# Routed experts on one core: where expert 0's early results are kept, when row numbers are converted, and VectorE's turns spread over layer 2

## The chip, the cores and the metric

The kernel runs on one core of one Trainium2 chip. The metric is the device time of one execution in microseconds (us); the median of several runs counts.

## What is computed

Three stages follow each other: sliding-window attention, a gated dense block, and a layer of eight experts of which each token uses one. The change lies in the last stage; there `x` has 2304 rows of 512, `w1[e]` is 512 x 1024 and `w2[e]` is 1024 x 512.

```python
logits = x @ w_gate
e_idx = np.argmax(logits, axis=1)
...
for e in range(E):
    mask = e_idx == e
    h = np.maximum(x[mask] @ w1[e], 0.0)
    ye = h @ w2[e]
    out[mask] = gate_w[mask, None] * eom[mask, e, None] * ye
```

## The kernel before

Every product of two float32 matrices is made from three matmuls: each operand is split into a rounded high part and a low remainder (ScalarE writes the high part, line 470 or 771, VectorE or GpSimd the remainder, line 471 or 775), and high*high, high*low and low*high are summed. So ScalarE and VectorE must split every piece of weights and every block of rows before TensorE can use it.

The router scatters the rows of `x` by expert into a DRAM buffer `xs`, from tiles of a pool `mo` (line 434, indirect DMAs that GpSimd issues). Each expert has a stretch of `xs`; a row carries 512 numbers, its target row in `out` and its weight.

**Expert 0** begins before all rows are routed. Its first 256 rows were fetched early; `static_block` (line 1073) computes layer 1 (`hps`, line 1083) and then layer 2 (`mm2`, line 1053) in two blocks of 128 rows, `j` = 0 and 1. ScalarE scales each block's result into a tile from `y_first` (line 1179, shown in the trace as `gt`), and GpSimd issues an indirect DMA of 256 KB to `out` (line 1049). In a hook within the first block's matmuls, `rest` (line 1182) asks SyncE for the remaining rows of expert 0 (tile `xg`, 128 x 514) and for all four blocks of expert 1's rows (`rows`, line 818): eight DMAs of 128 KB, and one of 4 KB with row numbers and weights, which GpSimd converts to integers (line 804). A pair of row blocks lives in one of three buffers (`pair_tile`, line 792).

Then the pools `mo` and `moe` are closed (line 1195) and a pool `ex2` is opened in the same place in SBUF; `exT`, `hT` and `y` of all later experts live there. The remaining rows of expert 0 are transposed by TensorE (`gps`, line 841), split into `exT`, and go through `row_block` (line 1117): 24 matmuls of layer 1 with the rows as the stationary side (`rps`, line 1136), transposes (`tps`), and 24 matmuls of layer 2.

**Experts 1 to 7** each run a `static_block` of 288 columns: layer 1 is 96 matmuls, layer 2 48. While expert e computes, VectorE and ScalarE prepare e+1: eight weight pieces (`esplit`, line 778, one ScalarE copy and one VectorE subtraction each), and three row blocks, each turned by VectorE (line 850, into a PSUM bank of `ps_s`) and split (lines 470 and 471) into `exT`. `begin` and `turn` (lines 1207 to 1213) take the next row block from a list. ScalarE's and VectorE's order is the order in which the program is written (`manual_schedule`), and hooks after the matmuls of step f of layer 1 (`at1`), of the first block of layer 2 (`at2`) and of the second (`at3`) place this work in it; SyncE's and GpSimd's order around it is a scheduler's. After the two blocks an expert with more than 288 rows runs row blocks, one with 257 to 288 rows runs `few_rows` (line 1101, `yps` of line 1107), one with at most 256 goes straight on.

Of the kernel before, what the change touches and what calls it, by code (L numbers as in the profile page):

```python
# [9 lines left out]
F32 = mybir.dt.float32  # L10
# [11 lines left out]
NT, DM, DF, NE = B * S, H * D, 1024, 8  # L22
NP = H // 2
UNIT = 384
# [4 lines left out]
NS = NT + 128  # L29
# [412 lines left out]
def attention_moe_moe_kernel(ctx: ExitStack, tc: tile.TileContext, q0, k0, v, w1, w2, w3, w_out,  # L442
# [26 lines left out]
    def split(src, hi, lo, low=nc.vector):  # L469
        nc.scalar.activation(out=hi, in_=src, func=AF.Copy)  # L470
        low.tensor_tensor(lo, src, hi.bitcast(F32), op=ALU.subtract)  # L471
# [54 lines left out]
    raw, f32s, bits = {}, {}, {}  # L526
# [87 lines left out]
    mo, ghl = [None], [None]  # L614
# [125 lines left out]
    def eslot(e, i):  # L740
        if ew[e][i] is None:
            j = 0 if e % 2 == 0 else 2 + 2 * i
            ew[e][i] = [wslot(j), wslot(j + 1)]
        return ew[e][i]
# [4 lines left out]
    def eload(to):  # L749
        while nload[0] < min(to, len(items)):  # L750
            e, i, c = items[nload[0]]
            if ex[0] is not None and nload[0] % 4 == 3:
                t = ex[0].tile([128, 1024], F32, name="ck3", tag="ck3", bufs=1)
            else:
                t = exp_state["p"].tile([128, 1024], F32, name="ck2", tag="ck2", bufs=3)
            if i == 0:
                nc.sync.dma_start(out=t, in_=ew1[e, 128 * c:128 * c + 128, :])
            else:
                nc.sync.dma_start(out=t.rearrange("p (a d) -> p a d", a=2),
                                  in_=ew2[e, 256 * c:256 * c + 256, :].rearrange("(a p) d -> p a d", p=128))  # L760
            eq.append(t)
            nload[0] += 1
# [7 lines left out]
    def ehigh():  # L770
        nc.scalar.activation(out=eparts()[0], in_=eq[0], func=AF.Copy)  # L771

    def elow(low=V):
        hi, lo = eparts()
        low.tensor_tensor(lo, eq.popleft(), hi.bitcast(F32), op=ALU.subtract)  # L775
        nsplit[0] += 1

    def esplit(low=V):
        if nsplit[0] < len(items):
            ehigh()  # L780
            elow(low)
            eload(nsplit[0] + (3 if ex[0] is None else 4))
# [7 lines left out]
    idx, xg, xTs = {}, {}, {}  # L790

    def pair_tile():
        return exp_state["p"].tile([128, 1024], F32, name="xg", tag="xg", bufs=3)

    def blocks(t, r, n):

        o = t.rearrange("p (j c) -> p j c", c=128)
        for b in range(4):
            nc.sync.dma_start(out=o[32 * b:32 * b + 32],
                              in_=xs[r:r + 128 * n, 128 * b:128 * b + 128].rearrange("(j p) c -> p j c", p=32))  # L800

    def fetch_index(raw, i, r, n):
        nc.sync.dma_start(out=raw[:, 0:n], in_=xs[r:r + 128 * n, DM:RW].rearrange("(j p) t -> p j t", p=128))
        nc.gpsimd.tensor_copy(i[:, 0:n], raw[:, 0:n, 0])
# [6 lines left out]
    def index(e, pool=None, tag="idx", bufs=5):  # L811
        p = pool or exp_state["p"]
        t = p.tile([128, 12], F32, name="idx", tag=tag, bufs=bufs)
        raw = t[:, 4:12].rearrange("p (j t) -> p j t", t=2)
        idx[e] = (t[:, 0:4].bitcast(I32), raw[:, :, 1])
        return raw

    def rows(e):

        raw = index(e)  # L820
        for j in (0, 2):
            t = pair_tile()
            blocks(t, NS * e + 128 * j, 2)
            xg[e, j], xg[e, j + 1] = t[:, 0:512], t[:, 512:1024]
        fetch_index(raw, idx[e][0], NS * e, 4)

    def early_rows():

# [15 lines left out]
    def xT_block(g, xT, c0, ab=False):  # L844
        split(g_turn(g, ab), xT[:, 0, :, c0:c0 + 128], xT[:, 1, :, c0:c0 + 128])

    def xT_square(g, xT, c0):

        ps = ps_s.tile([128, 512], F32, name="gps", tag="S")
        V.transpose(out=ps, in_=g)  # L850
        h, lo = [xT[:, b, :, c0:c0 + 128].rearrange("p c (a j) -> p c a j", a=4) for b in range(2)]
        split(ps.rearrange("p (a c j) -> p c a j", a=4, c=4), h, lo)

    def early_turn(j):
        if j == 0:
# [197 lines left out]
    def mm2(hT, c0, w, hooks={}):  # L1053
        ps = ps_acc.tile([128, 512], F32, name="yps", tag="acc")
        for f in range(8):
            for i, (a, b) in enumerate(PASSES):
                mm(ps, lhsT=hT[f][a][:, c0:c0 + 128], rhs=w[b][:, 512 * f:512 * f + 512],  # L1057
                   start=f == 0 and i == 0, stop=f == 7 and i == 2)
            if f in hooks:
                hooks[f]()  # L1060
        return ps
# [55 lines left out]
    def row_block(xT, ix, j, w1e, w2e, own, then={}):  # L1117
        hs, hT = [], {}

        def turn(z):  # L1120
            tp = ps_s.tile([128, 512], F32, name="tps2", tag="S")
            for f in range(4):
                nc.tensor.transpose(tp[:, 128 * f:128 * f + 128], hs[z][:, 128 * f:128 * f + 128], ident)
            tp = tp.rearrange("p (a b) -> p a b", a=4)
            for f in (0, 2):
                h2 = own[4 * (j % 2) + 2 * z + f // 2][4][:, 0:512].rearrange("p (a b c) -> p a b c", a=2, b=2)
                split(tp[:, f:f + 2, :], h2[:, 0], h2[:, 1])
                for i in range(2):
                    hT[4 * z + f + i] = h2[:, 0, i], h2[:, 1, i]

        for z in range(2):
            ps = (ps_s if z else ps_v).tile([128, 512], F32, name="rps", tag="S" if z else "pv")
            for kk in range(4):
                c = 1024 * kk + 512 * z
                for i, (a, b) in enumerate(PASSES):
                    mm(ps, lhsT=xT[:, a, kk, 0:128], rhs=w1e[b][:, c:c + 512],
                       start=kk == 0 and i == 0, stop=kk == 3 and i == 2)
                if z and kk == 1:
                    turn(0)
            h = ex[0].tile([128, 512], F32, name="hs", tag="y", bufs=3)  # L1140
            nc.scalar.activation(out=h, in_=ps, func=AF.Relu)
            hs.append(h)
        ps = mm2(hT, 0, w2e, {1: lambda: turn(1), **then})
        emit_out(ps, ix, j)
# [25 lines left out]
    hold = {}  # L1170
# [6 lines left out]
        return h[:, 0], h[:, 1]  # L1177

    def y_first():
        return mo[0].tile([128, 2, UNIT], F32, name="gt", tag="gt", bufs=2).rearrange("p a b -> p (a b)")[:, 0:DM]  # L1180

    def rest():

        n0 = nc.values_load(rt.done[0:1, 0:1], min_val=0, max_val=256)
        index(0)
        xg[0, 0] = pair_tile()[:, 0:RW]
        nc.sync.dma_start(out=xg[0, 0], in_=xs[bass.ds(n0, 128), :])
        rows(1)

    at1 = {k: lambda n=n: step(n) for k, n in {(0, 2): 1, (1, 0): 1, (1, 2): 1, (2, 0): 1, (2, 2): 1, (3, 0): 3, (4, 3): 3, (5, 0): 3}.items()}  # L1190
    at1.update({f: lambda: esplit(nc.gpsimd) for f in ((0, 0), 1, (2, 1))})
# [12 lines left out]

    steps = deque()

    def turn():
        if steps:
            xT_square(*steps.popleft())

    def begin(e):
        steps.extend(prep(e))
        turn()

    w1e, w2e = eslot(0, 0), eslot(0, 1)
    n0 = nc.values_load(rt.done[0:1, 0:1], min_val=0, max_val=256)
    n = nc.values_load(rt.cnt[0:1, 0:1], min_val=0, max_val=NT)
    xT = ex[0].tile([128, 2, 4, 384], F32R, name="exT", tag="exT", bufs=2)[:, :, :, 256:384]
    own = [h_tile(f) for f in range(8)]
# [3 lines left out]
    written = ExitStack()  # L1223
    written.enter_context(tc.manual_schedule(engines={E.DVE, E.Activation}))
    xT_block(xg[0, 0], xT, 0)
    row_block(xT, idx[0], 0, w1e, w2e, own, {2: lambda: begin(1), 4: turn, 6: turn})
    for e in range(1, NE):
        at1 = {f: esplit for f in (0, 2, 4, 6)}
        at3 = {3: esplit, 6: esplit}
        if e + 1 < NE:  # L1230
            rows(e + 1)
            at3.update({0: lambda e=e: begin(e + 1), 2: turn, 5: turn})
        reg = {}

        def ahead():
            reg["n"] = nc.values_load(rt.cnt[0:1, e:e + 1], min_val=0, max_val=NT)  # L1236
            reg["lots"] = reg["n"] > EW

        def tell(label, cond):
            tc.mark_branch_hint_location(label, hint=cond, engines={E.PE})  # L1240

        at2 = {1: esplit, 2: ahead, 5: esplit, 7: lambda: tell(f"lots{e}", reg["lots"])}
        hT = static_block(e, idx[e], at1, at2, at3)
        w1e, w2e = eslot(e, 0), eslot(e, 1)
        n, lots = reg["n"], reg["lots"]
        xT = xTs.pop((e, 2))
        with tc.If(lots, label=f"lots{e}") as rest_of:
            more = n > 384
            tell(f"more{e}", more)
            row_block(xT[:, :, :, 256:384], idx[e], 2, w1e, w2e, hT, {3: lambda: xT_square(xg[e, 3], xT, 0)})  # L1250
            with tc.If(more, label=f"more{e}"):  # L1251
                row_block(xT, idx[e], 3, w1e, w2e, hT)
                with tc.If(n > 512):  # L1253
                    row_loop(e, 512, n, w1e, w2e, xT, hT)
        with rest_of.Else():
            with tc.If(n > 256):
                few_rows(hT, idx[e], w2e)
# [55 lines left out]
```

## Time and profile before

| what | value |
|---|---|
| three runs | 744.34, 745.35, 746.1 us |
| median | 745.35 us |
| the profiled execution | 742.05 us |
| its span, first to last instruction | 740.1 us |
| TensorE (PE) busy | 703.5 us, 95% |
| VectorE (DVE) / ScalarE (ACT) busy | 396.0 us, 54% / 306.4 us, 41% |
| GpSimd (POOL) busy | 152.4 us, 21% |
| the same page's clock row | full, but for two slices of 40 near 480 to 520 us |

Times in the trace are us from the start of the span. In a line of the timeline stand: start, duration, engine, source line, operation, out<-in, count, and in brackets how long the engine was idle before and what ended that. SPq is SyncE's DMA queue, PEq the sequencer of TensorE.

### The profile page before, as it was taken

The page shows a single profiled execution, that of the slowest core. Times are in us where ns is not written, and L with a number is a line of the kernel's source. Part 1 is how long each engine was busy: PE and PEld are TensorE (multiplying, and loading weights), DVE is VectorE, ACT ScalarE, POOL GpSimd, SP SyncE. Part 2 cuts the span into 40 slices and gives each one's busy share as a digit, 9 for nine tenths or more (in the row PEclk, how much of TensorE's full clock was granted, in tenths as well). Part 3 has the DMA queues.
Part 4 walks back from the last instruction along what each step waited for, and adds up shares of the span by engine and source line. Part 5 has one row for each costly group of instructions (what it writes and reads, how often), then busy time and mean ns, then how long its engine had stood idle before and what let it go on. Part 6 is the DMA issues. An engine that isn't in the chain of part 4 may idle for free. (4 is left out here: it accounts for less than half of the span.)

```text
span 740.1 us, 12043 instructions
## 1 busy us (share of the span) xinstructions
PE 703.5 (95%) x4423; PEld 627.8 (85%) x4423; DVE 396.0 (54%) x882; ACT 306.4 (41%) x707; POOL 152.4 (21%) x183
## 2 busy tenths in 40 slices
PE   7999999999999999999999999928999999999996
PEld 3788899999999999999999999816997988978985
DVE  7999788214544657364422425603666665566310
ACT  3665656222333435334412215402555554545222
POOL 4764655100310312030010012410011001010111
PEclk9999999999999999999999999968999999999999
DMA  9992699920211432122310024573576876474000
GB/s 355 408 407 92 222 323 265 253 91 0 93 50 33 128 118 96 33 76 86 114 44 0 1 72 122 179 192 82 168 206 197 249 207 200 125 215 138 18 28 30
DMA packets 53285, 105.80 MB, mean 143 GB/s; under 512 B 8524, under 2 KB 22860, under 8 KB 53200
## 3 DMA queue, kind: packets, MB, share of 16 engines
q1 hardware_dynamic: 49952, 95.24, 41.6%
q0 software_dynamic: 3104, 9.46, 3.4%
q8 instruction: 45, 0.74, 0.4%
q14 instruction: 40, 0.33, 0.1%
q10 hardware_dynamic: 144, 0.03, 0.0%
HBM read 86.83 MB, written 18.53 MB: 142 GB/s over the span
## 5 line engine op out<-in xcount | busy, mean ns | idle before, releaser
L622 PE MATMUL ab<-xt,w 128*128 128x384 f32 x1152 | 216.4, 340 | 0.0
L622 PEld LDWEIGHTS ab<-xt,w 128*128 128x128 f32 x1152 | 199.5, 188 | 2.1
L646 PE MATMUL acc<-w,gt 128*128 128x512 f32 x432 | 110.4, 400 | 0.0
L1057 PE MATMUL yps<-w,hT 128*128 128x512 f32 x432 | 101.0, 391 | 0.0
L1057 PEld LDWEIGHTS yps<-w,hT 128*128 128x128 f32 x432 | 80.4, 188 | 16.3
L646 PEld LDWEIGHTS acc<-w,gt 128*128 128x128 f32 x432 | 78.8, 188 | 15.2 <-DVE gt L638 0.2
L630 DVE TENSOR_TENSOR a_sb<-ab,a_sb 128x384 f32<-128x384 f32 x48 | 26.7, 555 | 89.8 <-PE ab L622 84.5
L191 ACT ACTIVATE pp<-sps,nm 128x128 f32<-128x128 f32 x144 | 46.7, 365 | 53.0 <-DVE nm L180 49.0
L213 POOL TENSOR_TENSOR pp<-pp,r 128x384 f32<-128x384 f32 x48 | 40.1, 850 | 118.7 <-DVE r L206 82.6
L775 DVE TENSOR_TENSOR w<-ck,w 128x1024 fp32r<-128x1024 f32 x45 | 54.5, 1224 | 14.0 <-ACT w L771 13.5
L1083 PE MATMUL hps<-exT,w 128*128 128x288 f32 x384 | 53.5, 300 | 5.2 <-ACT exT L470 4.3
L1083 PEld LDWEIGHTS hps<-exT,w 128*128 128x128 f32 x384 | 52.2, 192 | 7.1 <-ACT exT L470 5.1
L1049 POOL DMA_INDIRECT out<-y,idx x18 | 19.2, 1065 | 179.8 <-ACT exT L470 83.9
L771 ACT ACTIVATE w<-ck 128x1024 fp32r<-128x1024 f32 x48 | 49.9, 1055 | 6.7 <-DMA ck<-in_moe_w 6.0
L602 PE MATMUL wps<-w,w3T 128*128 128x512 f32 x192 | 50.3, 405 | 1.2 <-POOL w3T L593 1.0
L634 ACT ACTIVATE gt<-a_sb 128x384 fp32r<-128x384 f32 x48 | 25.1, 522 | 55.7 <-DVE a_sb L630 55.7
L627 ACT ACTIVATE a_sb<-ab 128x384 f32<-128x384 f32 x48 | 23.6, 491 | 55.2 <-PE ab L622 55.2
L1090 DVE SCALAR_TENSOR_TENSOR hT<-hps,hT 128x256 fp32r<-128x256 f32 x112 | 29.1, 301 | 28.4 <-ACT hT L1088 26.5
L1083 PE MATMUL hps<-exT,wx 128*128 128x288 f32 x288 | 41.2, 304 | 3.2 <-ACT exT L470 2.6
L1083 PEld LDWEIGHTS hps<-exT,wx 128*128 128x128 f32 x288 | 40.2, 195 | 4.6 <-ACT exT L470 3.4
L602 PEld LDWEIGHTS wps<-w,w3T 128*128 128x128 f32 x192 | 34.4, 188 | 9.7 <-POOL w3T L593 1.9
L1088 ACT ACTIVATE hT<-hps 128x288 fp32r<-128x288 f32 x56 | 23.0, 411 | 46.2 <-PE hps L1083 44.5
(155 smaller groups left out, 915.6 us busy)
## 6 DMA issues: line engine op xcount, KB each, us to landing
ck<-in_moe_w SPq DMA_DIRECT2D x80, 512.0 KB
q<-in_q SPq DMA_DIRECT2D x16, 576.0 KB
v<-in_v SPq DMA_DIRECT2D x16, 576.0 KB
xs<-x SPq DMA_DIRECT2D x32, 257.0 KB
w<-in_moe_w SPq DMA_DIRECT2D x16, 512.0 KB
xg<-xs SPq DMA_DIRECT2D x56, 128.0 KB
k<-in_k SPq DMA_DIRECT2D x16, 320.0 KB
w<-in_moe_w_out SPq DMA_DIRECT2D x8, 512.0 KB
```

The costliest lines, as they stand in the source:

```text
L191: nc.scalar.activation(out=p[:, o], in_=ps[:, o], func=AF.Exp, bias=nm[:, i:i + 1], scale=0.125, **(dict(accum_out=s["rs"][:, 3 * g + i:3 ...
L213: nc.gpsimd.tensor_tensor(p, p, s.pop(("r", g)).unsqueeze(2).to_broadcast([128, 3, 128]), op=ALU.mult)
L602: mm(ps, lhsT=t[:, a, 128 * j:128 * j + 128], rhs=wo[b][:, o:o + 512], start=g == 0 and j == 0 and x == 0, stop=g == 1 and j == 3 and x == 2)
L622: mm(ps, lhsT=w[a][:, c:c + 128], rhs=x[:, b, kk, :], start=kk == 0 and i == 0, stop=kk == 3 and i == 2)
L630: V.tensor_tensor(asb[u, m], gps.pop((u, m, 1)), asb[u, m], op=ALU.mult)
L634: nc.scalar.activation(out=g[:, 0, :], in_=asb[u, m], func=AF.Copy)
L646: mm(accs[u][t], lhsT=g[:, a, 128 * t:128 * t + 128], rhs=ws["w34"][b][:, 512 * m:512 * m + 512], start=m == 0 and i == 0, stop=m == 7 and ...
L771: nc.scalar.activation(out=eparts()[0], in_=eq[0], func=AF.Copy)
L775: low.tensor_tensor(lo, eq.popleft(), hi.bitcast(F32), op=ALU.subtract)
L1057: mm(ps, lhsT=hT[f][a][:, c0:c0 + 128], rhs=w[b][:, 512 * f:512 * f + 512], start=f == 0 and i == 0, stop=f == 7 and i == 2)
L1083: mm(ps[:, 0:W], lhsT=w1e[a][:, c:c + 128], rhs=xT[:, b, kk, 0:W], start=kk == 0 and i == 0, stop=kk == 3 and i == 2)
L1090: nc.vector.scalar_tensor_tensor(out=lo, in0=ps[:, o], scalar=0.0, in1=h[0][:, o].bitcast(F32), op0=ALU.max, op1=ALU.subtract)
```

## The change

Five edits go together.

1. `y_first` takes one pair tile of the pool of row tiles (128 x 1024, both early results) in place of tiles of `mo`. That pool stays open when `mo` closes.
2. `rows` takes one pair of blocks at a time and no longer asks for the row numbers. `rest` asks for expert 1's first pair alone; the second pair, in the buffer of the early results, and the numbers are asked for after expert 0's remaining rows were split.
3. `numbers` fetches and converts row numbers, after both pairs.
4. Expert 1's first two blocks are turned and split ahead of expert 0's row block, the third in the hook at f=2 of its layer 2 (before: all three, at f=2, 4 and 6).
5. For experts 2 to 7 the three turns move from `at3` (f = 0, 2, 5) to `at2` f=1, `at2` f=5 and `at3` f=1, each with a weight split between the turn and the split of its block. The two weight splits of `at3` move from f=3 and 6 to f=1 and 5.

```diff
-    def rows(e):
-        raw = index(e)
-        for j in (0, 2):
-            t = pair_tile()
-            blocks(t, NS * e + 128 * j, 2)
-            xg[e, j], xg[e, j + 1] = t[:, 0:512], t[:, 512:1024]
-        fetch_index(raw, idx[e][0], NS * e, 4)
+    def rows(e, j):
+        if j == 0:
+            index_of[e] = index(e)
+        t = pair_tile()
+        blocks(t, NS * e + 128 * j, 2)
+        xg[e, j], xg[e, j + 1] = t[:, 0:512], t[:, 512:1024]
+    def numbers(e):
+        fetch_index(index_of[e], idx[e][0], NS * e, 4)
...
     def y_first():
-        return mo[0].tile([128, 2, UNIT], F32, name="gt", tag="gt", bufs=2).rearrange("p a b -> p (a b)")[:, 0:DM]
+        if "y" not in hold:
+            hold["y"] = pair_tile()
+            return hold["y"][:, 0:DM]
+        return hold["y"][:, DM:2 * DM]
...
-        rows(1)
+        rows(1, 0)
...
-    def turn():
-        if steps:
-            xT_square(*steps.popleft())
     def begin(e):
         steps.extend(prep(e))
-        turn()
+    def turn(n=1, sp=False):
+        todo = [steps.popleft() for _ in range(n)]
+        ps = [square(t[0]) for t in todo]
+        if sp:
+            esplit()
+        for p, t in zip(ps, todo):
+            halves(p, *t[1:])
...
     xT_block(xg[0, 0], xT, 0)
-    row_block(xT, idx[0], 0, w1e, w2e, own, {2: lambda: begin(1), 4: turn, 6: turn})
+    rows(1, 2)
+    numbers(1)
+    begin(1)
+    turn(2)
+    row_block(xT, idx[0], 0, w1e, w2e, own, {2: turn})
...
-        at3 = {3: esplit, 6: esplit}
+        at3 = {1: esplit, 5: esplit}
         if e + 1 < NE:
-            rows(e + 1)
-            at3.update({0: lambda e=e: begin(e + 1), 2: turn, 5: turn})
+            rows(e + 1, 0)
+            rows(e + 1, 2)
+            numbers(e + 1)
+            begin(e + 1)
+            at3[1] = lambda: turn(1, True)
...
-        at2 = {1: esplit, 2: ahead, 5: esplit, 7: lambda: tell(f"lots{e}", reg["lots"])}
+        at2 = {1: esplit, 2: ahead, 5: esplit} if e + 1 == NE else {1: lambda: turn(1, True), 2: ahead, 5: lambda: turn(1, True)}
```

`square` is VectorE's turn and `halves` the two splits, which stood together in `xT_square`.

**GpSimd at the end of expert 0.** The first two rows take the row numbers from expert 0's remaining rows, line 804 converts an expert's numbers, and the line below it with `out` sends the two early results. Before:

```order
L808 CAST idx<-xg 128x1
L809 COPY idx<-xg 128x1
L804 CAST idx<-idx 128x4
L1049 DMA out<-gt,idx 2304x512 x2
L804 CAST idx<-idx 128x4
L1216 TENSOR_LOAD done
```

Now:

```order
L808 CAST idx<-xg 128x1
L809 COPY idx<-xg 128x1
L1059 DMA out<-xg,idx 2304x512 x2
L1232 TENSOR_LOAD done
L1236 REGISTER_ALU
```

The conversion of expert 1's numbers no longer stands ahead of the early results, nor expert 2's behind them; both now come after the branch.

**SyncE from expert 0's remaining rows (line 1187, now 1200) to expert 2's first weights.** `ck` are weight pieces, `xg` row blocks, `idx` numbers. Before, ahead of the branch:

```order
L1187 DMA xg<-xs 128x514
L799 DMA xg<-xs 32x8x128 x8
L803 DMA idx<-xs 128x4x2
L757 DMA ck_5104<-in_moe_w 128x1024
L757 DMA ck_5117<-in_moe_w 128x1024
L757 DMA ck_5130<-in_moe_w 128x1024
L803 DMA idx<-xs 128x4x2 x2
```

Now, ahead of the branch and (from the second `x4` on) behind it:

```order
L1200 DMA xg<-xs 128x514
L799 DMA xg<-xs 32x8x128 x4
L757 DMA ck_5097<-in_moe_w 128x1024
L757 DMA ck_5110<-in_moe_w 128x1024
L757 DMA ck_5123<-in_moe_w 128x1024
...
L799 DMA xg<-xs 32x8x128 x4
L803 DMA idx<-xs 128x4x2
L799 DMA xg<-xs 32x8x128 x8
L803 DMA idx<-xs 128x4x2
L757 DMA ck_5473<-in_moe_w 128x1024
```

Expert 1's second pair and its numbers moved behind three weight pieces and the branch, and both pairs of expert 2 now stand ahead of the weight piece `ck_5473`, which came first there.

**VectorE in layer 2 of expert 1.** Before:

```order
L775 TENSOR_TENSOR w_5616<-ck_5475,w_5615 128x1024
L1236 TENSOR_LOAD cnt
L775 TENSOR_TENSOR w_5616<-ck_5513,w_5615 128x1024
L850 STREAM_TRANSPOSE gps<-xg 128x512
L471 TENSOR_TENSOR exT<-gps,exT 128x4x128
L850 STREAM_TRANSPOSE gps<-xg 128x512
L471 TENSOR_TENSOR exT<-gps,exT 128x4x128
L775 TENSOR_TENSOR w_5616<-ck_5551,w_5615 128x1024
L850 STREAM_TRANSPOSE gps<-xg 128x512
L471 TENSOR_TENSOR exT<-gps,exT 128x4x128
L775 TENSOR_TENSOR w_5616<-ck_5589,w_5615 128x1024
```

Now:

```order
L854 STREAM_TRANSPOSE gps<-xg 128x512
L775 TENSOR_TENSOR w_5618<-ck_5475,w_5617 128x1024
L471 TENSOR_TENSOR exT<-gps,exT 128x4x128
L1259 TENSOR_LOAD cnt
L854 STREAM_TRANSPOSE gps<-xg 128x512
L775 TENSOR_TENSOR w_5618<-ck_5513,w_5617 128x1024
L471 TENSOR_TENSOR exT<-gps,exT 128x4x128
L854 STREAM_TRANSPOSE gps<-xg 128x512
L775 TENSOR_TENSOR w_5618<-ck_5551,w_5617 128x1024
L471 TENSOR_TENSOR exT<-gps,exT 128x4x128
L775 TENSOR_TENSOR w_5618<-ck_5589,w_5617 128x1024
```

Each turn now stands ahead of a weight split and its block's split behind it, and the first turn is ahead of all four weight splits of the layer.

## Rows read from the trace of the kernel before

**Rows 1.** Waits of TensorE: us in total, times, longest.

```profile
PE rps L1136 <- ACT exT L470: 14.3, 1, 14.3
PE hps L1083 <- ACT exT L470: 6.9, 4, 3.0
```

**Rows 2.** Timeline of all engines, end of expert 0.

```profile
480.33 4.33 SPq L799 DMA_DIRECT2D xg<-xs  x8
...
482.68 0.69 ACT L1048 ACTIVATE gt<-yps,idx 128x512 f32<-128x512 f32 x1 [2.26 <-PEq L1220]
483.00 0.19 POOL L808 CAST idx<-xg 128x1 int32<-128x1 f32 x1 [8.11 <-DMA xg<-xs]
...
483.08 0.63 PE L841 MATMUL gps<-ident,xg 128*128 128x128 f32 x4 [0.52 <-DMA xg<-xs]
...
489.17 0.19 POOL L804 CAST idx<-idx 128x4 int32<-128x4 f32 x1 [5.86 <-DMA idx<-xs]
489.93 1.01 POOL L1049 DMA_INDIRECT out<-gt,idx  x1 [0.57 <-issue]
494.45 0.98 POOL L1049 DMA_INDIRECT out<-gt,idx  x1 [3.51 <-DMA out<-gt,idx]
...
497.31 0.60 ACT L470 ACTIVATE exT<-gps 128x512 fp32r<-128x512 f32 x1 [13.95 <-DMA out<-gt,idx]
```

**Rows 3.** Timeline of TensorE, experts 1 to 6 and one row block.

```profile
514.51 0.55 PE L1083 MATMUL hps<-exT,w 128*128 128x288 f32 x1 [3.00 <-ACT exT L470]
...
529.11 11.06 PE L1057 MATMUL yps<-w,hT 128*128 128x512 f32 x48
...
556.44 11.08 PE L1057 MATMUL yps<-w,hT 128*128 128x512 f32 x48
...
582.15 11.05 PE L1057 MATMUL yps<-w,hT 128*128 128x512 f32 x48
...
609.52 11.08 PE L1057 MATMUL yps<-w,hT 128*128 128x512 f32 x48
620.44 4.36 PE L1136 MATMUL rps<-wx,exT 128*128 128x512 f32 x18
...
633.02 12.91 PE L1083 MATMUL hps<-exT,w 128*128 128x288 f32 x96 [0.43 <-PEq L1251]
645.77 11.06 PE L1057 MATMUL yps<-w,hT 128*128 128x512 f32 x48
...
671.62 11.05 PE L1057 MATMUL yps<-w,hT 128*128 128x512 f32 x48
```

**Rows 4.** One stretch: length, TensorE busy, granted clock, DMA share, GB/s.

```profile
498.00:503.50 5.50, 5.50 (x18) 0.73 0.88 192
```

**Rows 5.** Timeline of SyncE's queue: two loads of row blocks.

```profile
511.87 1.79 SPq L799 DMA_DIRECT2D xg<-xs  x4
...
544.04 3.32 SPq L799 DMA_DIRECT2D xg<-xs  x5
```

**Rows 6.** A stretch: length, PE, PEld, DVE, ACT, POOL busy, clock, DMA share, GB/s.

```profile
515.50:516.00 0.50, 0.50 (x3) 0.50 (x4) 0.00 (x0) 0.00 (x0) 0.50 (x1) 0.50 0.00 0
```

**Rows 7.** Groups by line: turns and splits, busy us and mean ns.

```profile
L775 DVE TENSOR_TENSOR w<-ck,w 128x1024 fp32r<-128x1024 f32 x45 | 54.5, 1224 | 14.0 <-ACT w L771 13.5 <-issue 0.4
L771 ACT ACTIVATE w<-ck 128x1024 fp32r<-128x1024 f32 x48 | 49.9, 1055 | 6.7 <-DMA ck<-in_moe_w 6.0 <-PE ab L622 0.8
L471 DVE TENSOR_TENSOR exT<-gps,exT 128x512 fp32r<-128x512 f32 x24 | 16.6, 692 | 41.7 <-ACT exT L470 41.7
L850 DVE STREAM_TRANSPOSE gps<-xg 128x512 f32<-128x512 f32 x23 | 16.5, 718 | 0.0
L470 ACT ACTIVATE exT<-gps 128x512 fp32r<-128x512 f32 x24 | 14.3, 596 | 40.0 <-DVE gps L850 21.9 <-DMA out<-gt,idx 13.9 <-issue 4.2
```

**Rows 8.** Timeline of layer 2 of expert 2: copy of the third block.

```profile
568.16 0.60 ACT L470 ACTIVATE exT<-gps 128x512 fp32r<-128x512 f32 x1 [1.93 <-DVE gps L850]
```

**Rows 9.** Waits of SyncE's queue: us in total, times, longest.

```profile
SPq L757 <- DMA out<-gt,idx: 8.1, 1, 8.1
```

More of the change, by code (lines that the diff above doesn't have):

```diff
@@ L816, in index @@
         return raw
-    def rows(e):
-        raw = index(e)
-        for j in (0, 2):
-            t = pair_tile()
-            blocks(t, NS * e + 128 * j, 2)
-            xg[e, j], xg[e, j + 1] = t[:, 0:512], t[:, 512:1024]
-        fetch_index(raw, idx[e][0], NS * e, 4)
+    def rows(e, j):
[6 more added lines that the diff above has]
+        fetch_index(index_of[e], idx[e][0], NS * e, 4)
+    index_of = {}
     def early_rows():
@@ L845, in xT_block, with square, halves, xT_square @@
         split(g_turn(g, ab), xT[:, 0, :, c0:c0 + 128], xT[:, 1, :, c0:c0 + 128])
-    def xT_square(g, xT, c0):
+    def square(g):
         ps = ps_s.tile([128, 512], F32, name="gps", tag="S")
         V.transpose(out=ps, in_=g)
+        return ps.rearrange("p (a c j) -> p c a j", a=4, c=4)
+    def halves(ps, xT, c0):
         h, lo = [xT[:, b, :, c0:c0 + 128].rearrange("p c (a j) -> p c a j", a=4) for b in range(2)]
-        split(ps.rearrange("p (a c j) -> p c a j", a=4, c=4), h, lo)
+        split(ps, h, lo)
+    def xT_square(g, xT, c0):
+        halves(square(g), xT, c0)
     def early_turn(j):
@@ L1240, in tell @@
             tc.mark_branch_hint_location(label, hint=cond, engines={E.PE})
-        at2 = {1: esplit, 2: ahead, 5: esplit, 7: lambda: tell(f"lots{e}", reg["lots"])}
+        at2 = {1: esplit, 2: ahead, 5: esplit} if e + 1 == NE else {1: lambda: turn(1, True), 2: ahead, 5: lambda: turn(1, True)}
+        at2.update({7: lambda: tell(f"lots{e}", reg["lots"])})
         hT = static_block(e, idx[e], at1, at2, at3)
```

## The prediction

> **What bounds the kernel now.** TensorE is busy 95% of the span by the page's first part, so I first ask where it stands still, in the view of the waits. Two lines hold nearly all of it [rows 1]: one wait of 14.3 us of `rps`, the first matmul of expert 0's row block, and four waits of 6.9 us together of `hps`, the first matmul of a layer 1. Both wait for ScalarE's copy into `exT`. The next view is the timeline around the long wait [rows 2]. TensorE's transposes of expert 0's remaining rows end at 483.08 + 0.63 = 483.71, but the ScalarE copy that reads them begins at 497.31, and what ended its wait is named: the DMA from `gt` to `out`, an early result. The reader should follow that back. The tile of the copy lies in the pool opened over the closed one, so it can't be written before the early results have left. They left late: ScalarE had written them by 482.68 + 0.69 = 483.37, but GpSimd issued the first at 489.93, because ahead of it in GpSimd's queue stood the conversion of expert 1's row numbers (489.17), which waited 5.86 us for its load. The second went out only when the first had landed, 4.52 us later, and landed 2.86 us after that.
>
> The third view is the timeline of TensorE alone [rows 3]. With no wait, layer 2 and layer 1 of a 288-column expert take 620.44 - 609.52 = 10.92 and 645.77 - 633.02 = 12.75, together 23.67 us from one layer 2 to the next. The short waits stand at the starts of experts 1, 3, 4 and 6; behind experts 1, 4 and 6 a `few_rows` or a row block hides the preparation of the next. The last view is the granted clock [rows 4]: 0.73 on the mean in the 5.5 us after the long wait, that is partly the lower level of 1.2 GHz, so a wait costs more than its own length.
>
> **The change part by part.** Expected from here: the start of `hps` of expert 1 (514.51), then its layer 1, then the transitions.
>
> *Early results in an open pool, conversions later.* The wait of the copy for the early results goes. Next in line are TensorE's transposes (483.71) and ScalarE's second early result (483.37), then a branch on ScalarE whose cost no row shows. TensorE took the same branch and began its transposes 0.4 us after its sequencer had released ScalarE (482.68 to 483.08 [rows 2]); between 0 and 0.9 I take 0.3 past 483.71. So the copy begins near 484.0, takes 0.60, and TensorE starts at 484.65.
>
> The row block takes 12.15 us at the full clock (633.02 - 0.43 - 620.44). But two turns and splits of expert 1 now stand ahead of it on VectorE and ScalarE, and its second half writes into a PSUM bank that the first of them uses. It comes after 12 of 24 matmuls, 484.65 + 12 x 0.24 = 487.5. The first turn needs its rows: four DMAs from 480.33 [rows 2]. Four such DMAs elsewhere were issued from 511.87 on, and by 515.5 no data moved [rows 5, 6], so 4.0 us from first issue to landing; with the 257 KB copy ahead of them I take 485.0. At worst it is 489.17, when the numbers loaded behind them were in. Two turns and two splits, alternating, then end at 485.3 + 2 x 0.72 + 2 x 0.69 = 488.1, the first split at 487.5 [rows 7]: no wait, or up to 3.6 us at worst. The ScalarE copy of the row block's own result is due behind them at 487.5 and is not late.
>
> The third block is loaded into the buffer of the early results, so SyncE must wait until both have landed. GpSimd issues the first at 483.4 (after the conversion at 483.00), the second 4.5 us later, and that lands 2.9 to 4.5 us later: 490.8 to 492.4, I take 491.3. Four loads land 4.0 us after, 495.3; turn 0.72, copy 0.60 and subtraction 0.69 make the block's two parts ready at 496.7 and 497.4. The row block ends at 484.65 + 12.15 = 496.8. So `hps` runs properly from 497.3 instead of 514.51: **17.2 us**, at least 12, at most 18. The Trainium skill (DMA: Bandwidth & Descriptors, section Anatomy of one DMA — SWDGE (gpsimd) path) gives 2.0 us and bytes over 436e3 for such a copy: by an estimate from it, 2.6 us for each early result, and the third block would be ready 2.8 us sooner, so that the row block's end alone counts and the gain is 17.7. The rows' 4.52 and 2.86 are longer, and I keep them.
>
> Behind that wait SyncE now holds the other loads: 1 index load, 8 blocks and the weight piece `ck_5473`. At 0.45 us of issue each (1.79 for four [rows 5]) that piece is issued at about 497.5. Its split is the last of four in expert 1's layer 1, some 11 us after 497.3, so this costs nothing; if the wait were 8 us longer it would begin to. The numbers of expert 1 are needed when its first block leaves, 18 us after 497.3.
>
> *Expert 1's layer 1* took 529.11 - 514.51 = 14.6, against 12.75 without the lower clock [rows 3]: **1.85 us**, none if TensorE still pauses there.
>
> *Turns spread over layer 2.* The three transitions without cover, from layer 2 to next layer 2, took 582.15 - 556.44 = 25.71, 609.52 - 582.15 = 27.37 and 671.62 - 645.77 = 25.85 [rows 3], 2.04, 3.70 and 2.18 over 23.67: **7.9 us** in all. The third block's copy ended at 568.16 + 0.60 = 568.76 there [rows 8], 12.3 after the layer's start. Now, from that start: VectorE is free at about 1.7, after the last weight split of layer 1 (1.22) and some 0.5 for the last `hT`; each of three rounds is a turn, a weight split and a block's split, 0.72 + 1.22 + 0.69 = 2.63 [rows 7], and ScalarE's 1.06 + 0.60 for a round fit beside it, its copy of the first output (due at 5.6) too. Three rounds end at 9.6, before the layer's 10.92, and the fourth weight split follows at 10.9, where nobody waits yet. So all of the excess should go; between 0 and 7.9 I take 7.9. The cover of this is the rows' early landing: the first turn is now wanted at 1.7, ahead of the weight splits. The loads of the block wanted first at 558.1 were issued from 544.04 to 547.36 [rows 5] and land 2.3 us after the last issue, 549.6, so 8.5 us are left.
>
> No arithmetic and no DMA is added.
>
> **The sum.** 17.2 + 1.85 + 7.9 = 27.0 us. The profiled execution took 742.05, its span 740.1; it becomes 715.0. The median of the runs shown is 3.3 above the profiled one, and I subtract the same from it: 745.35 - 27.0 = 718.4 us.
>
> **The rivals.**
>
> *The row block is late.* The first rows land near their bound of 489.17, or the early results take 4.5 us each and the third block comes late, and the clock falls again. For it: DMA queues are full in this stretch, and the third block's chain ends within 0.6 us of the row block's. Cost 3 to 6 us: 721 to 724.
>
> *The spread turns don't pay.* VectorE's row is in order; if something else there is late, the transitions stay as they are: 745.35 - 19.1 = 726.3. Against it: 1.3 us of slack in the sum above.
>
> *The change doesn't do what it says:* the copy into `exT` still waits, for the routed rows' scatter that also leaves the closed pool. Then 17.2 and 1.85 go, but for the third block's 3.0: 745.35 - 7.9 - 3.0 = 734.5. Against it: the load of the remaining rows, which reads what that scatter wrote, was already in at 483.00 [rows 2].
>
> *Slower: SyncE's queue holds the rows.* Place: the first turn in `at2`, in each of the six transitions. A SyncE load that waits for a buffer holds all loads behind it; it waited 8.1 us in one piece for the early results [rows 9]. If rows come after the turn is wanted, VectorE stands, the weight splits behind the turn stand with it, and TensorE waits for both. It decides from 8.5 + 1.3 = 9.8 us later than in the trace on; to eat 27.0 and 1.5 more over six transitions each must be 4.8 beyond that: about 747 us. For it: the turns are wanted earlier, and the loads have moved behind weight pieces. Against it: the weight splits also end earlier, and their loads with them. The Trainium skill (DMA: Bandwidth & Descriptors, section Anatomy of one DMA — SWDGE (gpsimd) path) says that a wait on a semaphore is held by the issuing sequencer before dispatch, which is this mechanism; by that the trace's 8.1 us agree.
>
> **How the numbers follow.** The forecast has 0.72, by itself 715.5 to 721. The late row block has 0.12, the turns that don't pay 0.08, the copy that still waits 0.05, slower 0.03. The range reaches from 714.5 (18 in place of 17.2, a lower clock nowhere, and some 2 us of spread between runs) to 726.5, which takes in the first two rivals and leaves out 0.08 and the tails. No change means within 0.2% of 745.35, about what a measurement of this kernel can tell; only mixtures with the last rival fall there, 0.02. So faster 0.95, slower 0.03.
>
> **What would show it.** Right: TensorE's list of waits has no `rps` entry above 1 us; GpSimd issues the first early result near 483.4; `hps` of expert 1 starts near 497; the clock stays full from 480 to 525; the starts of layer 2 of experts 2, 3 and 4 lie 23.7 apart; the chain's tail is as long as before. Wrong: a wait of `rps` on VectorE's split, of VectorE's turn on a DMA in layer 2, or of a weight split on its piece.

## The result, and the profile after

The changed kernel takes **723.68 us** (median of 6 runs, 722.26 to 725.11); the kernel before took 745.73 in the same comparison (6 runs, 742.43 to 747.35). The ratio is 0.9708, with an interval of 0.9681 to 0.9735: 22 us faster. The forecast of 718.4 was 5.3 too low; its range of 714.5 to 726.5 held the time. What came is the price of the first rival, the late row block (721 to 724). The profiled execution took 725.11, its span is 723.1, so by profile against profile the gain is 742.05 - 725.11 = 16.9; the profiled execution of before was 3.3 quicker than its median, that of the changed kernel 1.4 slower.

The page's first line, busy time by engine, has TensorE at 97% of a shorter span; the work itself is the same.

```profile
PE 703.1 (97%) x4423; PEld 628.5 (87%) x4423; DVE 393.8 (54%) x882; ACT 307.1 (42%) x707; POOL 151.8 (21%) x183
```

The long wait is gone from TensorE's list of waits, and what is left of the two entries of before [rows 1] is this:

```profile
PE hps L1093 <- ACT exT L470: 2.7, 1, 2.7
PE rps L1146 <- ACT exT L470: 1.5, 1, 1.5
PE rps L1146 <- DVE exT L471: 0.2, 1, 0.2
```

The timeline of all engines of the changed kernel at the end of expert 0 answers to [rows 2] (start, duration, engine, line, operation, and in brackets the idle time and what ended it):

```profile
482.16 1.90 SPq L799 DMA_DIRECT2D xg<-xs  x4
484.17 1.65 SPq L757 DMA_DIRECT2D ck<-in_moe_w  x3
484.50 0.69 ACT L1058 ACTIVATE xg<-yps,idx 128x512 f32<-128x512 f32 x1 [2.66 <-PEq L1236]
...
484.91 0.63 PE L845 MATMUL gps<-ident,xg 128*128 128x128 f32 x4 [0.50 <-DMA xg<-xs]
...
485.59 1.00 POOL L1059 DMA_INDIRECT out<-xg,idx  x1 [0.45 <-ACT xg L1058]
486.35 0.60 ACT L470 ACTIVATE exT<-gps 128x512 fp32r<-128x512 f32 x1 [1.16 <-PE gps L845]
...
488.38 1.32 DVE L854 STREAM_TRANSPOSE gps<-xg 128x512 f32<-128x512 f32 x2 [0.70 <-DMA xg<-xs]
...
493.67 0.98 POOL L1059 DMA_INDIRECT out<-xg,idx  x1 [7.08 <-ACT hT L470]
...
496.41 1.81 SPq L799 DMA_DIRECT2D xg<-xs  x4
...
501.21 0.73 DVE L854 STREAM_TRANSPOSE gps<-xg 128x512 f32<-128x512 f32 x1 [3.58 <-DMA xg<-xs]
```

ScalarE's copy into `exT` no longer waits for a DMA to `out`: it begins 0.81 after TensorE's transposes end (485.54). But the two early results, sent by GpSimd at 485.59 and 493.67, lie 8.08 us apart, where they lay 4.52 apart before [rows 2]. What ends the second one's wait there, by the trace's inference, is a ScalarE copy (`hT`) that had ended at 493.10. I read it as the first one's landing: the traces of before [rows 2] and of the closed pool below name that DMA at the same place. SyncE loads expert 1's third block behind both, from 496.41 on, and VectorE waits 3.58 us for it.

The timeline of TensorE alone, for [rows 3]:

```profile
502.62 16.13 PE L1093 MATMUL hps<-exT,w 128*128 128x288 f32 x96 [2.70 <-ACT exT L470]
518.58 11.06 PE L1067 MATMUL yps<-w,hT 128*128 128x512 f32 x48
...
545.91 11.08 PE L1067 MATMUL yps<-w,hT 128*128 128x512 f32 x48
...
559.12 11.22 PE L1093 MATMUL hps<-exT,w 128*128 128x288 f32 x84 [0.16 <-issue]
570.17 11.08 PE L1067 MATMUL yps<-w,hT 128*128 128x512 f32 x48
...
594.28 11.05 PE L1067 MATMUL yps<-w,hT 128*128 128x512 f32 x48
...
630.49 11.07 PE L1067 MATMUL yps<-w,hT 128*128 128x512 f32 x48
...
654.59 11.04 PE L1067 MATMUL yps<-w,hT 128*128 128x512 f32 x48
```

And stretches of TensorE (length, busy, granted clock, DMA share, GB/s): from the copy to the row block's end, the pause, and expert 1's layer 1.

```profile
486.00:490.50 4.50, 3.33 (x12) 1.00 1.01 327
490.50:499.90 9.40, 9.38 (x44) 1.00 0.39 112
499.90:502.60 2.70, 0.01 (x1) 0.95 1.16 206
502.60:512.00 9.40, 9.27 (x47) 0.65 0.81 187
```

From these lines the gain splits as the prediction's sum did:

| piece | before | after | gain | forecast |
|---|---|---|---|---|
| start of `gps` | 483.08 | 484.91 | -1.83 | 0 |
| `gps` to `hps` of expert 1 | 31.43 | 17.71 | 13.72 | 17.2 |
| expert 1's layer 1 | 14.60 | 15.96 | -1.36 | 1.85 |
| three uncovered transitions | 78.93 | 72.47 | 6.46 | 7.9 |

The sum is 16.99, against 16.94 of the two executions. The first line lies ahead of the change: the last scatter of the routed rows is already issued 1.85 us later in this execution (474.74 against 472.89), and the kernels below have the start of `gps` between 483.1 and 484.9. The tail is as it was: from the last of these starts of layer 2 to the end of the span 68.5 in both.

### The profile page after: what moved, and what is told of

Same layout as the page of the kernel before. It is cut to its first block, busy times and chain, and to the rows that moved or that the text cites. A ratio compares the mean times of both kernels' runs of the same rounds, so it can differ in the third digit from the quotient of the medians.

```text
span 723.1 us, 12045 instructions
## 1 busy us (share of the span) xinstructions
PE 703.1 (97%) x4423; PEld 628.5 (87%) x4423; DVE 393.8 (54%) x882; ACT 307.1 (42%) x707; POOL 151.8 (21%) x183
## 5 line engine op out<-in xcount | busy, mean ns | idle before, releaser
L775 DVE TENSOR_TENSOR w<-ck,w 128x1024 fp32r<-128x1024 f32 x45 | 54.7, 1217 | 12.6 <-ACT w L771 12.2
L602 PE MATMUL wps<-w,w3T 128*128 128x512 f32 x192 | 52.5, 419 | 2.3 <-ACT w3T L589 1.3
L1059 POOL DMA_INDIRECT out<-y,idx x18 | 17.6, 976 | 161.2 <-ACT y L1058 110.2
L602 PEld LDWEIGHTS wps<-w,w3T 128*128 128x128 f32 x192 | 36.1, 197 | 11.3 <-POOL w3T L593 1.9
L168 PE MATMUL sps<-k,q 128*128 128x128 f32 x288 | 40.5, 280 | 1.1 <-DMA k<-in_k 1.1
L168 PEld LDWEIGHTS sps<-k,q 128*128 128x128 f32 x288 | 38.0, 194 | 3.9 <-issue 1.7
```

Source lines behind the costliest of these rows:

```text
L168: nc.tensor.matmul(ps[:, 128 * i:128 * i + 128], lhsT=s["q"][:, 128 * c:128 * c + 128], rhs=s["k"][:, 64 * c:64 * c + 128], start=late, st ...
L602: mm(ps, lhsT=t[:, a, 128 * j:128 * j + 128], rhs=wo[b][:, o:o + 512], start=g == 0 and j == 0 and x == 0, stop=g == 1 and j == 3 and x == 2)
```

## The experiments

Theory after the result: the open pool and the spread turns work as forecast, and what is missing comes from the first early result, which takes long to land because SyncE's loads, now issued around it, share the DMA engines with it. Expert 1's third block is loaded behind it, so TensorE pauses and its clock falls. Rivals: the landing time is the scatter's own; the pool is not what matters; the spread turns don't pay.

All runs in one table. Issue is when GpSimd issued the two early results; the last three columns are pieces of the profile, as above. The first four were compared with 745.23 (median of 13 runs), the last four with 746.04 (9 runs).

| kernel | median us | ratio [interval] | issue of results | `gps` to `hps` | layer 1 | transitions |
|---|---|---|---|---|---|---|
| before | 745.73 | | 489.93, 494.45 | 31.43 | 14.60 | 78.93 |
| changed | 723.68 | 0.9708 [0.9681, 0.9735] | 485.59, 493.67 | 17.71 | 15.96 | 72.47 |
| late turns | 730.90 | 0.9794 [0.9751, 0.9838] | 483.91, 492.46 | 18.00 | 14.88 | 80.48 |
| closed pool | 729.11 | 0.9789 [0.9759, 0.982] | 483.82, 491.97 | 27.76 | 12.64 | 72.13 |
| conversions only | 744.04 | 0.9989 [0.9967, 1.001] | 485.00, 490.48 | 30.94 | 14.88 | 80.46 |
| other buffer | 717.24 | 0.9627 [0.9601, 0.9652] | 484.33, 493.15 | 14.85 | 12.64 | 72.12 |
| pieces later | 718.50 | 0.9643 [0.9621, 0.9664] | 484.00, 489.83 | 15.41 | 13.35 | 72.12 |
| results first | 718.54 | 0.9646 [0.9622, 0.9669] | 482.09, 488.21 | 16.06 | 12.64 | 72.13 |
| other buffer, results first | 718.15 | 0.9639 [0.9617, 0.9662] | 480.61, 486.39 | 16.02 | 12.63 | 72.13 |
| spread only | 736.95 | 0.9883 [0.9859, 0.9907] | 490.58, 495.13 | 32.82 | 14.89 | 72.50 |

### Late turns: the changed kernel without edit 5

```diff
-        at3 = {1: esplit, 5: esplit}
+        at3 = {3: esplit, 6: esplit}
-            at3[1] = lambda: turn(1, True)
+            at3.update({0: turn, 2: turn, 5: turn})
-        at2 = {1: esplit, 2: ahead, 5: esplit} if e + 1 == NE else {1: lambda: turn(1, True), 2: ahead, 5: lambda: turn(1, True)}
+        at2 = {1: esplit, 2: ahead, 5: esplit}
```

> The changed kernel with its fifth edit undone: the turns of experts 2 to 7 stand in at3 again (f=0, 2, 5) and the weight splits of at3 at f=3 and 6. If the spread is worth what the two profiles show, the three transitions without cover lie 25.7 to 27.4 us apart again in place of 24.2, and the time is 723.7 + 6.5 = 730.2 us (729 to 732). Rival: the spread moves nothing by itself, the transitions became shorter because the stretch ahead of them did; then 723.7 us (722.5 to 725).

730.90 us (726.21 to 731.38, 4 runs), 7.2 above the changed kernel. The waits of `hps` are back, four of them:

```profile
PE hps L1093 <- ACT exT L470: 5.9, 4, 2.0
```

One of 2.0 is expert 1's, the three others are the transitions, which take 80.48 in place of 72.47, 8.0 more. The stretch from `gps` to expert 1's layer 2 is 0.8 shorter here than in the changed kernel's profile, which leaves 7.2 by these pieces. The two profiled executions lie only 5.4 apart, as `gps` starts 1.7 earlier here.

### Closed pool: the changed kernel without edit 1

```diff
-        if "y" not in hold:
-            hold["y"] = pair_tile()
-            return hold["y"][:, 0:DM]
-        return hold["y"][:, DM:2 * DM]
+        return mo[0].tile([128, 2, UNIT], F32, name="gt", tag="gt", bufs=2).rearrange("p a b -> p (a b)")[:, 0:DM]
```

> The changed kernel with its first edit undone: the early results lie in tiles of the pool that closes; expert 1's second pair goes into the free buffer of the row tiles. If the pool's closing is what holds the copy into exT, the copy begins only when the second early result has landed: the first is issued 0.7 us after TensorE's transposes, the two take 7.4 to 10.9 us, so rps waits 8.5 to 12 us in place of 1.5, while the 2.7 us of hps and its lower clock go: 723.7 + 7 to 10.5 - 2.7 - 1 to 3 = 725 to 731 us. Rival: issuing the early results sooner (conversions later) is all that counts, and an open pool adds nothing: 723.7 us or below, rps waiting under 3 us.

729.11 us. Its timeline of GpSimd, ScalarE and TensorE shows the early results issued as soon as in the changed kernel, and the copy still waiting for them:

```profile
483.82 1.00 POOL L1059 DMA_INDIRECT out<-gt,idx  x1 [0.45 <-ACT gt L1058]
491.97 0.98 POOL L1059 DMA_INDIRECT out<-gt,idx  x1 [7.15 <-DMA out<-gt,idx]
...
496.21 0.60 ACT L470 ACTIVATE exT<-gps 128x512 fp32r<-128x512 f32 x1 [12.89 <-DMA out<-gt,idx]
...
496.86 3.35 PE L1146 MATMUL rps<-wx,exT 128*128 128x512 f32 x7 [13.10 <-ACT exT L470]
```

So the later conversions send the results 6 us sooner, and the wait of `rps` falls only from 14.3 to 13.1 (8.5 to 12 expected), since here too they lie 8.15 apart. The open pool is what takes the wait away, and with it 10.05 between `gps` and `hps`. The kernel is only 5.4 slower than the changed one, because the edit does a second thing: with the early results back in `mo`, expert 1's second pair finds a free buffer, and SyncE asks for it at 484.88 instead of 496.41. The third block is no longer late, `hps` begins without a wait and layer 1 takes 12.64. The pool by itself is therefore better priced against the other buffer below, where that pair is also loaded early: 729.11 - 717.24 = 11.9 us.

### Conversions only: the kernel before, with row numbers fetched later

```diff
-        fetch_index(raw, idx[e][0], NS * e, 4)
+        index_of[e] = raw
+    def numbers(e):
+        fetch_index(index_of[e], idx[e][0], NS * e, 4)
+    index_of = {}
...
     xT_block(xg[0, 0], xT, 0)
+    numbers(1)
...
             rows(e + 1)
+            numbers(e + 1)
```

> The kernel before with one thing changed: row numbers are fetched and converted after expert 0's remaining rows were split. If GpSimd's queue (the conversion ahead of the early results) is a part of the long wait, the first early result is issued some 6 us sooner and the rps wait falls from 14.3 to 8 to 11 us: 745.7 - 3.5 to 6.5 = 739 to 742 us. Rival: the early results land no sooner, as SyncE's loads share the DMA engines with them: 745.7 us, rps waiting over 13 us.

No change that can be measured, and a miss of the theory. The results go out at 485.00 and 490.48, but the copy still begins at 496.92, against 497.31 [rows 2], and `rps` waits 12.6: the second result needs 6.4 us to land. In its timeline of SyncE three weight pieces and four loads of expert 2's first rows are issued from 487.07 and from 489.24 on; before, those rows were asked for at 497.75. So this kernel moved loads beside the results too, and does not price GpSimd's order by itself.

### Other buffer: expert 1's second pair into the buffer of expert 0's remaining rows

```diff
-        xg[0, 0] = pair_tile()[:, 0:RW]
+        hold["x"] = pair_tile()
+        xg[0, 0] = hold["x"][:, 0:RW]
...
-        t = pair_tile()
+        t = hold["x"] if (e, j) == (1, 2) else pair_tile()
```

The early results' buffer then goes to expert 2's first pair.

> The changed kernel with one thing changed: expert 1's second pair is loaded into the buffer of expert 0's remaining rows, which TensorE has read by then, and not into that of the early results (which goes to expert 2's first pair). If the wait for the early results is what makes the third block late (2.7 us of hps, and the lower clock in the layer 1 behind it, 15.96 in place of 12.75 us), that load is issued within 3 us of TensorE's transposes, hps waits under 0.3 us and the time is 723.7 - 2.7 - 3.2 = 717.8 us (716.5 to 719.5). Rival: the DMA engines are full in this stretch, the third block lands no sooner and hps still waits over 1.5 us: 722 to 724.5 us.

717.24 us, faster than both kernels. Its timeline: the early results lie as far apart as in the changed kernel (8.82), but the second pair is loaded at 485.61, VectorE turns the third block at 496.28, and `hps` begins behind the row block without a wait.

```profile
484.33 1.00 POOL L1059 DMA_INDIRECT out<-xg,idx  x1 [0.45 <-ACTq L1237]
...
485.61 3.07 SPq L799 DMA_DIRECT2D xg<-xs  x4
...
493.15 0.98 POOL L1059 DMA_INDIRECT out<-xg,idx  x1 [7.82 <-ACT hT L470]
...
496.28 0.72 DVE L854 STREAM_TRANSPOSE gps<-xg 128x512 f32<-128x512 f32 x1
```

```profile
498.50 12.80 PE L1093 MATMUL hps<-exT,w 128*128 128x288 f32 x96
```

That the third block waits for the early results costs 17.71 + 15.96 - 14.85 - 12.64 = 6.2 us by these pieces, and 6.4 by the medians.

### Pieces later: three weight pieces of expert 2 behind expert 1's second pair

```diff
+    def split_only():
+        ehigh()
+        elow()
...
-        static_block(0, idx["early"], at1, {0: rest, 1: esplit, 4: esplit, 7: esplit}, {}, h_first, y_first, 256)
+        static_block(0, idx["early"], at1, {0: rest, 1: split_only, 4: split_only, 7: split_only}, {}, h_first, y_first, 256)
...
-    rows(1, 2)
+    with tc.manual_schedule(engines={E.SP}):
+        rows(1, 2)
+        eload(nsplit[0] + 3)
```

> The changed kernel, but the three weight pieces of 512 KB that SyncE asks for right behind expert 1's first two row blocks (484.17 in the changed kernel) are asked for only behind expert 1's second pair. Theory, that the first early result takes 8.1 us to land because these loads share the DMA engines with it: the second early result is issued 4.5 to 6 us after the first (before: 4.5), hps of expert 1 waits at most 1 us, and the time is 718 to 721 us unless the late pieces hold up expert 1's layer 1, which would show as a wait of VectorE or ScalarE on a piece. Rival, that the 8.1 us are the scatter's own (its target rows, or its source in a 128 x 1024 buffer): the second is still issued about 8 us after the first, hps waits 2.7 us, and the time stays at 723 to 725 us.

718.50 us. GpSimd's and SyncE's rows:

```profile
484.00 1.00 POOL L1059 DMA_INDIRECT out<-xg,idx  x1 [0.45 <-issue]
...
489.83 0.98 POOL L1059 DMA_INDIRECT out<-xg,idx  x1 [4.83 <-ACT hs L1151]
```

```profile
492.57 1.81 SPq L799 DMA_DIRECT2D xg<-xs  x4
494.48 1.34 SPq L757 DMA_DIRECT2D ck<-in_moe_w  x3
```

Three pieces now come behind the third block, while the scheduler drew a later one forward, to 483.48, so 1 MB less stands beside the first result. It needs 5.83 in place of 8.08, and the rival of the source buffer falls too, as the closed pool's results, in tiles of `mo`, lie 8.15 apart; the third block's load is issued 9.25 us after the start of `gps` (changed: 11.50), and `hps` waits 0.94 and 0.33 (at most 1 expected) at the full clock. The late pieces hold nothing up: behind those waits layer 1 takes 12.78. The stretches of the DMA share say when the engines ran empty, in this kernel and then in the changed one (length, GpSimd busy, granted clock, DMA share, GB/s):

```profile
488.50:488.75 0.25, 0.00 (x0) 1.00 0.04 16
488.75:489.00 0.25, 0.00 (x0) 1.00 0.00 0
```

```profile
492.25:492.50 0.25, 0.00 (x0) 1.00 0.08 33
492.50:493.50 1.00, 0.00 (x0) 1.00 0.00 0
```

### Results first: GpSimd sends the first early result ahead of the remaining rows' numbers

```diff
-        index(0)
+        idx[0] = idx["early"]
```

> The changed kernel, but GpSimd issues the first early result before it takes the row numbers of expert 0's remaining rows (these are put into the same tile of numbers as the early ones, so their conversion comes behind that result). Expected in both theories: first issue near 482.3 in place of 485.6. Theory, that contention with SyncE's loads sets the landing: the early start wins 3.3 us or a little more, the second is issued by 490.4, hps of expert 1 waits under 0.5 us, layer 1 takes about 13 us, and the time is 718 to 720 us. Rival, that the loads drain first whatever stands ahead of them: the second is still issued near 493 (some 11 us after the first), and the time stays at 723 to 725 us.

718.54 us. The remaining rows' numbers go into the early rows' tile, so their conversion comes behind the first result:

```profile
482.09 1.27 POOL L1059 DMA_INDIRECT out<-xg,idx  x1 [5.49 <-ACT xg L1058]
484.83 0.19 POOL L809 COPY idx<-xg 128x1 f32<-128x1 f32 x1 [1.47 <-DMA xg<-xs]
...
487.46 0.19 POOL L808 CAST idx<-xg 128x1 int32<-128x1 f32 x1 [2.45 <-DMA out<-xg,idx]
488.21 0.99 POOL L1059 DMA_INDIRECT out<-xg,idx  x1 [0.56 <-issue]
```

Issued ahead of the weight pieces (483.91), the first result has landed by 487.46, 5.4 later. The second, issued among them, takes 5.4 itself: SyncE loads the third block at 493.59. `hps` waits no more. Something else is paid here: `rps` waited 1.58, VectorE's first turn 1.59 for its rows, and the clock was 0.50 behind it, so the row block's first 18 matmuls took 6.26 (4.86 in the kernel with the pieces later):

```profile
487.12 6.26 PE L1146 MATMUL rps<-wx,exT 128*128 128x512 f32 x18 [1.58 <-ACT exT L470]
```

```profile
488.50:491.50 3.00, 3.00 (x9) 0.50 0.88 350
```

### Other buffer and results first together

The edits of both kernels.

> The kernel in which expert 1's second pair goes into the buffer of expert 0's remaining rows (717.24 us), with the first early result issued ahead of those rows' numbers as well. Theory, that there nothing waits for the early results any more but expert 2's first pair, which is wanted only 25 us later: no change, 716.5 to 718 us. Rival, that the early results still hold SyncE's queue enough to cost something: 1 us or more faster than 717.24, with the row block's waits (0.9 and 0.7 us there) gone.

718.15 us (717.89 to 719.34, 5 runs), against 717.24 (716.64 to 717.51, 4 runs) without the second edit. The intervals of the ratios overlap: it wins nothing, and the median lies just above the expected 716.5 to 718. The lower clock in the row block is there as well: 1.78 of wait, then 5.99 for the 18 matmuls. So 717.24 us stays the lowest median.

### Spread only: the kernel before, with edit 5 alone

```diff
-        at3 = {3: esplit, 6: esplit}
+        at3 = {1: esplit, 5: esplit}
-            at3.update({0: lambda e=e: begin(e + 1), 2: turn, 5: turn})
+            begin(e + 1)
+            at3[1] = lambda: turn(1, True)
...
-        at2 = {1: esplit, 2: ahead, 5: esplit, 7: lambda: tell(f"lots{e}", reg["lots"])}
+        at2 = {1: esplit, 2: ahead, 5: esplit} if e + 1 == NE else {1: lambda: turn(1, True), 2: ahead, 5: lambda: turn(1, True)}
+        at2.update({7: lambda: tell(f"lots{e}", reg["lots"])})
```

> The kernel before with the spread turns alone (edit 5): experts 2 to 7 are turned at f=1 and 5 of the first block of layer 2 and f=1 of the second; results, loads and numbers as before. Theory, that this part stands by itself: the three uncovered transitions fall from 78.9 to 71.5 to 72.5 us in all, the wait of rps stays at 14 us, and the time is 737.5 to 739.5 us (745.4 less 6.5 to 7.9). Rival, that it needs the later row numbers and the new order of loads: VectorE's first turn waits for its rows in layer 2, the transitions stay above 76 us in all, and the time is 743 us or more.

736.95 us, just below the expected range: the transitions take 72.50, the wait of `rps` stays at 14.5. The part stands by itself. By the medians it wins 9.1 (6.9 to 10.5 by the interval), more than the 6.4 between the two profiles' transitions; by the profiled executions it is 4.5 (742.05 and 737.52). The paragraph on the spread turns below says where a part of this difference lies.

Two things were not run: the open pool with the conversions where they were, and the changed kernel without its fourth edit. What the conversions are worth beside the open pool, and what the earlier turns of expert 1 are worth, is therefore not shown.

## Why the prediction was right and wrong

*The number.* It was nearer than its working. The sum was made on the profiled execution and gave 715.0, where 725.11 was measured: 10 of its 27 us are missing. By the medians only 5 are missing, because the two profiled executions lie on opposite sides of their medians. That part is luck. Of the signs it named for being right, the transitions (24.1 to 24.3 for 23.7) and the tail came; `hps` near 497 (502.62), no `rps` wait above 1 us (1.5) and the full clock (0.65) did not.

*The pool and the order of GpSimd: right in kind.* The copy waits no more for a DMA, and the closed pool shows that this needs the pool, not the conversions. The first result went out 0.68 after the transposes' start, forecast 483.4 - 483.08 = 0.3.

*The step that failed* is the sentence "GpSimd issues the first at 483.4 ..., the second 4.5 us later". The 4.5 came from the trace of before, where the first result was issued at 489.93, and I carried it to an issue 6 us earlier, into the middle of SyncE's loads. It measured 8.08. The prediction said that DMA queues are full in this stretch and gave that 0.12; it should have been the forecast. The pieces later (5.83) and the results first (landed 5.4 after issue) show that the loads beside it set most of this time: the same 256 KB to the same rows in each. Whether these wait for each other in the DMA engines or in the memory behind them, no run separates. The second landed after 2.74, below the 2.9 to 4.5 forecast. The Trainium skill (DMA: Bandwidth & Descriptors, section Issuing engines are not separate DMA queues) says that transfers of SyncE and GpSimd run on the same 16 DMA engines and interleave; these traces agree: with the results first, the first had landed by 487.46 while the DMA share stood at 0.76 or more from 483 to 491. The prediction did not weigh it. The prediction's estimate of 2.6 us for each early result from the Trainium skill (DMA: Bandwidth & Descriptors, section Anatomy of one DMA — SWDGE (gpsimd) path) agrees with the 2.74 measured when the DMA engines were idle, and with no first result.

What followed from it: the load of the third block at 496.41, its turn at 501.21, and `hps` 2.70 late, then the granted clock of 0.65 on the mean from 502.6 to 512, between the levels of 1.2 and 2.4 GHz, so that layer 1 lost 1.36 where 1.85 was to be won. The other buffer gives all of it back: 12.64 for layer 1, and 717.24 us, near the forecast of 718.4, which had counted on 0.5 of wait there (497.3 - 496.8).

*Smaller terms of the same step.* The copy began 0.81 after the transposes in place of 0.3, within the bounds of 0 and 0.9; the first turn waited 0.70 for its rows and the row block 0.18 for its split; the row block took 12.9 instead of 12.15 at a granted clock of 1.00, and beyond that 0.18 its cause was not followed. So the 3.5 missing between `gps` and `hps` (13.72 for 17.2) are 2.2 of waiting beyond the 0.5, 0.8 of the row block and 0.5 ahead of it. By its own terms, two of the sum's figures are 0.1 too high: the third block's parts come to 496.6 and 497.3, and its estimate of 2.8 sooner to 2.7.

*Expert 1's layer 1: the condition failed.* The 1.85 was said to be none if TensorE still pauses; it was worse than none. In the kernels without a pause it measured 12.63 and 12.64, so 2.0 was there to win.

*The spread turns: right.* VectorE's three turns of expert 2's layer 2 stand 1.57, 3.91 and 6.24 after its start (forecast: 1.7, then every 2.63):

```profile
547.48 0.72 DVE L854 STREAM_TRANSPOSE gps<-xg 128x512 f32<-128x512 f32 x1
549.82 0.70 DVE L854 STREAM_TRANSPOSE gps<-xg 128x512 f32<-128x512 f32 x1
552.15 0.70 DVE L854 STREAM_TRANSPOSE gps<-xg 128x512 f32<-128x512 f32 x1
```

TensorE no longer waits for ScalarE at these transitions. Each keeps 0.43 to 0.59 over the 23.67 of the covered ones, which is the whole difference between 7.9 and 6.46; 0.16 of it is an idle gap that ends on "issue", the rest was not followed. The floor, taken from transitions behind a row block or `few_rows`, was that much too low for these. One number of before was also low: its transition from 556.44 took 25.71 [rows 3], the same one in the two other traces with the old turns (late turns, conversions only) 27.25. Against those two the spread wins 8.0. The clock makes this difference. In the trace of before, expert 3 and expert 4 begin behind the same two waits:

```profile
568.81 0.40 PE L1083 MATMUL hps<-exT,w 128*128 128x288 f32 x1 [1.29 <-ACT exT L470]
569.54 12.78 PE L1083 MATMUL hps<-exT,w 128*128 128x288 f32 x95 [0.33 <-DVE exT L471]
...
594.50 0.40 PE L1083 MATMUL hps<-exT,wx 128*128 128x288 f32 x1 [1.29 <-ACT exT L470]
595.23 14.46 PE L1083 MATMUL hps<-exT,wx 128*128 128x288 f32 x95 [0.33 <-DVE exT L471]
```

The granted clock is 1.00 through the first of these layers and 0.89 on the mean of the second, from 594.5 to 609.5. In the two other traces it is expert 3's layer too that loses the clock (14.32 and 14.31 in place of 12.78). So the 7.9 held about 1.5 of lower clock beside the waits, which the prediction did not name, and in two of the three traces it was lost once more. This may be part of why the profiled execution of before lies 3.3 below the median; that is argued, not shown.

*The slower rival did not come:* no turn of the changed kernel waits for its rows behind the one at 501.21, and expert 2's pairs, asked for from 498.87 on, are turned from 520.22 on without a wait.

## What to carry to other kernels

A landing time read from a trace belongs to the queues at that moment: when a transfer is moved to an earlier place, ask what else is in flight there before the old duration is used again. Who waits for a slow transfer can often be chosen: giving the early results' buffer to expert 2's first pair, asked for at 495.88 and turned only at 512.78 there, won at least as much (717.24) as making the results faster (718.5). And a part that costs little alone (2.7 us of waiting) should be priced with the lower clock that may follow it (here another 3.3).

## What was not expected of the hardware

The same indirect copy of 256 KB took 2.74, 4.52, 5.83, 8.08 and, in the kernel with the other buffer, 8.82 us from issue to the next one's release. In three traces the waiting GpSimd instruction went off 1.1 to 1.2 us after the DMA engines' share had fallen to 0: 492.5 to 493.67 (changed), 488.75 to 489.83 (pieces later), and before:

```profile
489.93:493.25 3.32, 1.01 (x1) 0.50 0.93 304
493.25:494.45 1.20, 0.00 (x1) 0.50 0.00 0
```

The engines need not be empty for it: in the closed pool the second result went off at 491.97 with a DMA share of 1.26 in the half microsecond around it.

The clock also fell behind short waits: `rps` waited 1.58 with the results first and 1.78 with both edits, and the row block ran at the lower level; with the pieces later it waited 1.20, with the other buffer 0.89 and 0.74, and the clock stayed full. But the length of the wait does not tell which: in the changed kernel `rps` waited 1.47 and the clock stayed at 1.00, with the late turns it waited 1.42 and the clock was at 0.50 from 486.5 to 488, with 6.16 for the 18 matmuls.

```profile
485.28 6.16 PE L1146 MATMUL rps<-wx,exT 128*128 128x512 f32 x18 [1.42 <-ACT exT L470]
```

The two layers of before shown above differ in the same way behind equal waits. The prediction had thought of the lower clock only behind the long wait and at `hps`.
